# Experts: a product moved into each arm's end, flips of h in another order, one subtraction moved to GpSimd

## The chip, the cores and the metric

The kernel runs on one core of a Trainium2 chip. The metric is the device time of one execution in microseconds (us); three runs of the kernel before give the median that is compared. The engines are TensorE (PE, matmuls), VectorE (DVE), ScalarE (ACT), GpSimd (POOL) and SyncE (SP, which issues most transfers).

## The reference

Three stages in a row, on 1792 tokens of 768 columns: attention with a sigmoid in place of the softmax; a mixture of eight experts, of which each token takes one or none; a dense layer with 2048 hidden columns. The change is in the experts:

```python
do_compute = (x @ w_skip) > 0
xc = x[do_compute]
e_idx = np.argmax(xc @ w_gate, axis=1)
gate_w = probs[np.arange(len(xc)), e_idx]      # softmax of the same logits
for e in range(8):
    mask = e_idx == e
    h = np.maximum(xc[mask] @ w1[e], 0.0)      # w1[e]: 768 x 1024
    y[mask] = gate_w[mask, None] * (h @ w2[e]) # w2[e]: 1024 x 768
out[do_compute] = xc + y
```

## The kernel before

**Stages.** Attention runs to about 199 us, the routing of tokens to about 208, the experts to about 464, the dense layer to the end at 946 us.

**Blocks.** The tokens of each expert are cut into blocks of up to 256 rows, two halves of P = 128. How many blocks there are and how full they are is known only at run time: `level(i, k)` branches on `kinds`. k = 3 is a whole block (both halves), k = 2 a "few" block (one half and FEW = 64 rows), k = 1 one half; k = 0 ends the chain in `close`. The program holds all three arms for every level; the input takes the kinds 3, 3, 2, 3, 2, 1, 1, 1 for blocks 0 to 7 and then `close`. An arm that isn't taken is passed by `rest`, one small operation on each of PE, ACT and DVE, at the join.

**Weights.** Each block streams eight chunks of 128x1536 fp32: chunks 0 to 3 are w1 (the way up), 4 to 7 are w2 (back; c4 and c6 hold rows for the first 384 columns of the output, c5 and c7 for the last 384, c4 and c5 for the first half of h, c6 and c7 for the second). `split_w` cuts each chunk into a high part (a cast on ACT, L728) and a low part (the difference on DVE, L730), which go to one of four buffers, chunk c to buffer c modulo 4. `ahead(i, c)` splits chunk c + 2 while chunk c is used. A product of fp32 operands is then three matmuls (`gemm`, L737 to L739): high by high, high by low, low by high. For 64 rows it is two (L801, L802).

**One block.** `columns` flips the gathered rows (twelve matmuls L138) into two banks pt0, pt1 and acc1, from which ACT (L762) and DVE (L763) make the high and low part of x. In `between` come the previous block's products c5 and c6 for its first half, and in `lead_in` c7; then the up products, from which `h_columns` flips h (L138, or L778 for 64 rows), and ACT (L785) and DVE (L786) take the relu's high and low part. `back` runs the products c4 to c7 (twelve matmuls each for 128 rows, eight for 64), `outcome` scales and adds them (L916; for 64 rows after a fold by two matmuls, L915). Products of the first half that follow a block's own arm run in the next level, behind the next block's flips, so that PE has work there. `slot_order` (L1040 to L1054, block 0 alone) makes the row order that later gathers use.

**Order.** PE, ACT and DVE run the instructions in the order of the code (`manual_schedule`); GpSimd and SP, which issue gathers (L711), scatters (L928) and the weight transfers, are ordered by a scheduler. An engine waits for the others through semaphores.

Of the kernel before, what the change touches and what calls it, by code (L numbers as in the profile page):

```python
# [23 lines left out]
P = 128  # L24
# [10 lines left out]
KF1 = F1 // P  # L35
# [6 lines left out]
N2 = DM // 2  # L42
WCH = 1536
FA = 9
TB = 4
NOR = NTT // TB * TB
# [43 lines left out]
def build(nc, tc, a):  # L90
# [3 lines left out]
    with ExitStack() as top:  # L94
# [77 lines left out]
        with ExitStack() as st:  # L172
# [238 lines left out]
            raw = load(0, 0, True)  # L411
# [246 lines left out]
        with ExitStack() as st:  # L658
# [60 lines left out]
                    for h in range(2)  # L719
                ]  # L720

            def split_w(i, c, hi=True, lo=True):
                if i == NB:
                    return
                j = 8 * i + c
                raw, w_hi, w_lo = raw_t[j % NRAW], whi_t[j % NSPL], wlo_t[j % NSPL]
                if hi:
                    nc.scalar.copy(w_hi, raw)  # L728
                if lo:
                    nc.vector.tensor_sub(w_lo, raw, w_hi)  # L730

            def weights(i, c):
                j = (8 * i + c) % NSPL
# [34 lines left out]
                    split_columns(g, ends[g], x2)  # L768

            def h_columns(nh, sizes):  # L770
                for h, n in enumerate(sizes):
                    pt = pt_t[(nh + h) % 2].rearrange("p (c n) -> p c n", c=4)[:, :, :n]
                    for j in range(4):
                        w = slice(j * P, (j + 1) * P)
                        if n == P:
                            flip(pt[:, j, :], hs_t[nh][:, w])
                        else:
                            nc.tensor.matmul(  # L778
                                pt[:, j, :], hf_t[nh][:, w], fold[:, :n], start=True, stop=True
                            )  # L780
                    f, t = slice(4 * nh, 4 * nh + 4), slice(h * P, h * P + n)
                    h_hi, h_lo = h2[:, 0, f, t], h2[:, 1, f, t]
                    if n < P:
                        h_lo = h2[:, 0, f, h * P + n : (h + 1) * P]
                    nc.scalar.activation(h_hi, pt, AF.Relu)  # L785
                    nc.vector.scalar_tensor_tensor(  # L786
                        h_lo, pt, 0.0, h_hi, op0=ALU.max, op1=ALU.subtract
                    )

            def product(o, h, n, a2, i, c, width, k0, total):  # L790

                t = slice(h * P, (h + 1) * P)
                for j in range(WCH // width):
                    w = slice(j * width, (j + 1) * width)
                    hi, lo = (u[:, w] for u in weights(i, c))
                    a_hi, a_lo = a2[:, 0, k0 + j, t], a2[:, 1, k0 + j, t]
                    first, last = k0 + j == 0, k0 + j == total - 1
                    if n == P:
                        gemm(o, a_hi, a_lo, hi, lo, first, last)
                    else:  # L800
                        nc.tensor.matmul(o, a_hi, hi, start=first, stop=False, skip_group_check=True)  # L801
                        nc.tensor.matmul(  # L802
                            o[:n], a_hi[:, :n], lo, start=False, stop=last, skip_group_check=True
                        )
# [52 lines left out]
                        else:  # L857
                            nc.scalar.copy(hf_t[nh], acc_t[(3, 0)[nh]])

            def back(i, h, n, chunks):  # L860

                for c in chunks:
                    c4, nh = divmod(c - 4, 2)
                    product(py[nh][h], h, n, h2, i, c, N2, 4 * c4, KF1)
                    if n < P and c4:
                        nc.scalar.copy(yf_t[nh], py[nh][h])

            def expert(i, sizes, following=None):
                whole = sizes == (P, P)
                aside = places_in_order() if i == 0 else iter(())  # L870

                def soon():
                    if i:
                        outcome(i - 1, 0, P)

                if i == 0:
                    split_w(0, 1)
                if whole:
                    up_two(i, aside, soon)
                    ahead(i, 4)  # L880
                else:
                    up_parts(i, sizes, aside, soon)
                    if len(sizes) > 1:
                        skips(f"many{i}")
                    elif i + 1 < NB:
                        skips(f"more{i + 1}", (following + 3) >> 2)
                ahead(i, 5)
                if i == 0:
                    run(aside)
                    order_rows()  # L890
                for h, n in list(enumerate(sizes))[1:]:
                    if whole:
                        back(i, h, n, range(4, 8))
                        outcome(i, h, n)
                        back(i, 0, P, range(4, 5))
                    else:
                        back(i, h, n, range(4, 6))
                        h_columns(1, sizes)
                        back(i, h, n, range(6, 8))
                        back(i, 0, P, range(4, 5))  # L900
                        outcome(i, h, n)
                if i == 0:
                    slot_order()
                if len(sizes) == 1:
                    back(i, 0, P, range(4, 5))
                    h_columns(1, sizes)

            def outcome(i, h, n):

# [46 lines left out]
            def between(i, more):  # L956

                if i == 0 and more:
                    return
                if i == 1 and not more:  # L960
                    gather(1)
                columns(i)
                if i == 0:
                    return
                back(i - 1, 0, P, range(5, 7))
                if more:
                    split_w(i, 0)
                    split_w(i, 1)
                else:
                    back(i - 1, 0, P, range(7, 8))  # L970
                    outcome(i - 1, 0, P)
                    scatter(i - 1)
# [62 lines left out]

            def slot_order():

                og = acc_t[1][:, :NOR]
                for t in range(NOR):
                    nc.tensor.matmul(  # L1040
                        og, one_hot[:, t], ca[:, t], start=(t == 0), stop=(t == NOR - 1)
                    )
                nc.vector.tensor_copy(order_off, og)
                for j in range(4):
                    nc.vector.scalar_tensor_tensor(
                        slot_off,
                        fill[:, 3 - j : NHB + 7 - j],
                        order_off[:, j : j + 1],
                        slot_off,
                        op0=ALU.mult,  # L1050
                        op1=ALU.add,
                    )
                nc.vector.tensor_scalar_add(slot_ext, slot_off, float(NT))
                nc.vector.tensor_scalar_add(order, order_off, float(NT))  # L1054
# [24 lines left out]
                nc.vector.tensor_copy(next(rest_t[1]), cst[:, :1])  # L1079

            def level(i, k):
                pass_on(i)
                if i == NB:
                    close(i)
# [262 lines left out]
```

## Time and profile before

| | us |
|---|---|
| runs shown | 947.25, 949.8, 951.26 |
| median | 949.8 |
| the profiled execution | 948.0 |
| its span | 946.2 |
| PE busy | 910.7 (96%) |
| DVE busy | 585.6 (62%) |
| ACT busy | 504.6 (53%) |
| GpSimd busy | 72.3 (8%) |

Times in the rows are counted from the start of the span. The busy share of PE is an average over stages. In the rows below, "idle before <-releaser" is the time for which the engine stood ahead of that instruction, and what it was waiting for last; "issue" there is time in which it waited for nothing that the profile shows. A matmul's duration overlaps that of the next; the step from start to start is what it costs in a row of them.

### The profile page before, as it was taken

Reading aid. Unit: us, or ns where it says so; the run is one execution under the profiler, and the core shown is the slowest. Engines: PE = TensorE matmul, PEld = TensorE weight load, DVE = VectorE, ACT = ScalarE, POOL = GpSimd, SP = SyncE. Lnnn points to the kernel's source line nnn. Section 1 sums busy time; section 2 is a strip of 40 time slices with the busy share of each in tenths; the row PEclk is TensorE's granted clock in tenths of the full one; section 3 lists DMA queues with packets and bytes.
Section 4 is the critical chain, followed back from the end, with each engine's and each line's share of the span. In section 5 each row is a group of like instructions: output and inputs, shape, how many; then the busy total and the mean of one; then the engine's idle time right before and its main releaser. Section 6 shows DMA issues by size and latency. Waiting matters only on the chain.

```text
span 946.2 us, 13964 instructions
## 1 busy us (share of the span) xinstructions
PE 910.7 (96%) x5331; PEld 754.2 (80%) x5331; DVE 585.6 (62%) x893; ACT 504.6 (53%) x703; POOL 72.3 (8%) x69
## 2 busy tenths in 40 slices
PE   7999999999999999999799999999999999999998
PEld 4555555549997898888799999888888888888997
DVE  3787877957656456688388888533443444434664
ACT  7777777535345346577254455434443434443664
POOL 0000000010220110234100000000000100000100
PEclk9999999999999999999999999999999999999999
DMA  9989887579962683594663333000010100000100
GB/s 247 266 254 269 248 272 228 168 242 417 357 258 70 251 295 111 207 410 174 222 201 100 104 101 113 34 34 1 17 34 17 55 13 1 1 1 1 68 1 34
DMA packets 33992, 139.50 MB, mean 147 GB/s; under 512 B 4874, under 2 KB 5514, under 8 KB 33890
## 3 DMA queue, kind: packets, MB, share of 16 engines
q1 hardware_dynamic: 29410, 119.17, 37.8%
q0 software_dynamic: 4480, 19.01, 5.8%
q8 instruction: 59, 0.97, 0.4%
q14 instruction: 43, 0.35, 0.1%
HBM read 117.58 MB, written 23.60 MB: 149 GB/s over the span
## 4 chain that ended last, share of the span: by engine, by line
PE 83%; DVE 3%; issue 2%; ACT 2%; DMA 1%; SPq 0%; ACTq 0%; DVEq 0%
PE acc L1220 15%; PE pt L1220 9%; PE acc L1187 8%; PE acc L1188 8%; PE acc L1189 8%; PE acc L737 6%; PE acc L738 6%; PE acc L739 6%; PE ps L239 3%; PE po L253 3%; PE pt L138 1%; PE acc L801 1%; PE acc L802 1%; PE acc L138 1%; DMA raw<-in_wi 1%
## 5 line engine op out<-in xcount | busy, mean ns | idle before, releaser
L730 DVE TENSOR_TENSOR wlo<-raw,whi 128x1536 fp32r<-128x1536 f32 x64 | 111.3, 1756 | 34.6 <-ACT whi L728 34.2
L1198 DVE SCALAR_TENSOR_TENSOR m<-m,acc 128x512 f32<-128x512 f32 (+1 forms) x64 | 39.7, 621 | 143.9 <-ACT m L1197 143.9
L1196 ACT ACTIVATE m<-acc 128x512 f32<-128x512 f32 (+1 forms) x64 | 34.9, 546 | 171.5 <-PE acc L1189 171.5
L1187 PE MATMUL acc<-x,wih 128*128 128x256 f32 (+1 forms) x360 | 121.1, 336 | 0.0
L1188 PE MATMUL acc<-x,wih 128*128 128x256 f32 (+1 forms) x360 | 121.1, 336 | 0.0
L1189 PE MATMUL acc<-x,wil 128*128 128x256 f32 (+1 forms) x360 | 120.7, 335 | 0.0
L728 ACT CAST whi<-raw 128x1536 fp32r<-128x1536 f32 x64 | 94.0, 1482 | 25.0 <-DMA raw<-in_w 9.1
L246 ACT ACTIVATE at<-ps,bias 112x896 f32<-112x896 f32 x96 | 89.1, 1009 | 29.1 <-PE ps L239 29.1
L1220 PE MATMUL acc<-wol,gh 128*128 128x256 f32 x320 | 101.0, 316 | 0.0
L1220 PE MATMUL acc<-woh,gl 128*128 128x256 f32 x320 | 100.5, 314 | 0.0
L1220 PE MATMUL acc<-woh,gh 128*128 128x256 f32 x320 | 100.4, 314 | 0.0
L253 PE MATMUL po<-at,vt 112*64 112x448 f32 x384 | 77.5, 545 | 0.7 <-DVE xT L261 0.7
L239 PE MATMUL ps<-qs,kh 128*112 128x448 f32 x192 | 73.3, 382 | 3.0 <-ACT kh L232 1.5
L1177 DVE TENSOR_TENSOR wol<-wo,woh 128x768 fp32r<-128x768 f32 x64 | 61.2, 956 | 23.4 <-ACT woh L1176 23.0
L239 PE MATMUL ps<-qs,kl 128*112 128x448 f32 x192 | 71.6, 373 | 2.6 <-DVE kl L233 2.6
L1189 PEld LDWEIGHTS acc<-x,wil 128*128 128x128 f32 x360 | 68.0, 189 | 7.4
L1187 PEld LDWEIGHTS acc<-x,wih 128*128 128x128 f32 x360 | 68.0, 189 | 6.3
L1188 PEld LDWEIGHTS acc<-x,wih 128*128 128x128 f32 x360 | 67.9, 189 | 5.9
L1220 PEld LDWEIGHTS acc<-woh,gh 128*128 128x128 f32 x320 | 60.3, 188 | 10.1
L1220 PEld LDWEIGHTS acc<-wol,gh 128*128 128x128 f32 x320 | 60.3, 188 | 9.3
L1176 ACT CAST woh<-wo 128x768 fp32r<-128x768 f32 x64 | 53.4, 834 | 26.0 <-PE acc L1220 25.9
L1202 DVE TENSOR_TENSOR gl<-m,gh 128x512 fp32r<-128x512 f32 (+1 forms) x64 | 40.0, 626 | 40.5 <-ACT gh L1201 40.5
(252 smaller groups left out, 2034.7 us busy)
## 6 DMA issues: line engine op xcount, KB each, us to landing
raw<-in_w SPq DMA_DIRECT2D x66, 768.0 KB, 10.6
kr<-in_k SPq DMA_DIRECT2D x22, 448.0 KB, 6.7
raw<-in_wi SPq DMA_DIRECT2D x9, 768.0 KB, 6.8
raw<-in_wo SPq DMA_DIRECT2D x9, 768.0 KB, 6.5
vt<-in_v SPq DMA_DIRECT2D x12, 448.0 KB, 6.3
x_d<-xr SPq DMA_DIRECT2D x14, 384.0 KB, 3.4
raw<-in_wi SPq DMA_DIRECT2D x14, 384.0 KB, 3.1
raw<-in_wo SPq DMA_DIRECT2D x14, 384.0 KB, 3.1
```

What stands on the lines that cost most here:

```text
L239: nc.tensor.matmul(ps[:CP, j, :S], kk[:, 2 * p + j, c * CP : (c + 1) * CP], qs[:, p, j], start=(i == 0), stop=(i == 1),)
L246: nc.scalar.activation(at[:, :, c, :], ps[:CP, :, :S], AF.Sigmoid, bias=bias[:CP], scale=QK_SCALE)
L253: nc.tensor.matmul(po[64 * j : 64 * j + 64, :S], vt[:, 2 * (hp % 2) + j, c, :], at[:, j, c, :], start=(c == 0), stop=(c == NCH - 1),)
L728: nc.scalar.copy(w_hi, raw)
L730: nc.vector.tensor_sub(w_lo, raw, w_hi)
L737: nc.tensor.matmul(o, a_hi, b_hi, start=first, stop=False)
L738: nc.tensor.matmul(o, a_hi, b_lo, start=False, stop=False)
L1177: nc.vector.tensor_sub(pair[1], wo_r[f], pair[0])
L1187: nc.tensor.matmul(o, a, b, start=(cc == 0), stop=False)
L1188: nc.tensor.matmul(o, a, c, start=False, stop=False)
L1189: nc.tensor.matmul(o, wil[:, cc], b, start=False, stop=(cc == KD - 1))
L1220: nc.tensor.matmul(o, a, b, start=(clears and f == 0 and k_ == 0), stop=(f == KF2 - 1 and k_ == 2), skip_group_check=True,)
```

## The change

- In each arm, c5's product for the first half moves from `between` of the next level (behind the next block's flips) to the arm's end. `between` then has c6 alone; `lead_in` keeps c7. In a few block c5's matmuls stand half ahead of and half behind the two folds.
- `h_columns` goes through the halves in reversed order. In a few block it moves behind c4 of both halves, and c5 of the 64 rows follows it, where both c4 and c5 of the 64 rows stood ahead of it.
- `slot_order` runs ahead of c4 and c5 (whole) or right behind c4, and uses acc0.
- The low part of chunk 7 isn't made by DVE in the arm; GpSimd makes it at the start of the next level, ahead of that level's gathers and scatters. Only chunk 7's product for the first half comes behind it.

```diff
--- before.py
+++ after.py
@@ -719,7 +719,7 @@
                     for h in range(2)
                 ]
 
-            def split_w(i, c, hi=True, lo=True):
+            def split_w(i, c, hi=True, lo=nc.vector):
                 if i == NB:
                     return
                 j = 8 * i + c
@@ -727,7 +727,7 @@
                 if hi:
                     nc.scalar.copy(w_hi, raw)
                 if lo:
-                    nc.vector.tensor_sub(w_lo, raw, w_hi)
+                    lo.tensor_sub(w_lo, raw, w_hi)
 
             def weights(i, c):
                 j = (8 * i + c) % NSPL
@@ -768,7 +768,7 @@
                     split_columns(g, ends[g], x2)
 
             def h_columns(nh, sizes):
-                for h, n in enumerate(sizes):
+                for h, n in reversed(list(enumerate(sizes))):
                     pt = pt_t[(nh + h) % 2].rearrange("p (c n) -> p c n", c=4)[:, :, :n]
                     for j in range(4):
                         w = slice(j * P, (j + 1) * P)
@@ -787,10 +787,10 @@
                         h_lo, pt, 0.0, h_hi, op0=ALU.max, op1=ALU.subtract
                     )
 
-            def product(o, h, n, a2, i, c, width, k0, total):
+            def product(o, h, n, a2, i, c, width, k0, total, part=slice(None)):
 
                 t = slice(h * P, (h + 1) * P)
-                for j in range(WCH // width):
+                for j in range(WCH // width)[part]:
                     w = slice(j * width, (j + 1) * width)
                     hi, lo = (u[:, w] for u in weights(i, c))
                     a_hi, a_lo = a2[:, 0, k0 + j, t], a2[:, 1, k0 + j, t]
@@ -857,11 +857,11 @@
                         else:
                             nc.scalar.copy(hf_t[nh], acc_t[(3, 0)[nh]])
 
-            def back(i, h, n, chunks):
+            def back(i, h, n, chunks, part=slice(None)):
 
                 for c in chunks:
                     c4, nh = divmod(c - 4, 2)
-                    product(py[nh][h], h, n, h2, i, c, N2, 4 * c4, KF1)
+                    product(py[nh][h], h, n, h2, i, c, N2, 4 * c4, KF1, part)
                     if n < P and c4:
                         nc.scalar.copy(yf_t[nh], py[nh][h])
 
@@ -884,26 +884,31 @@
                         skips(f"many{i}")
                     elif i + 1 < NB:
                         skips(f"more{i + 1}", (following + 3) >> 2)
-                ahead(i, 5)
+                ahead(i, 5, lo=None)
                 if i == 0:
                     run(aside)
                     order_rows()
-                for h, n in list(enumerate(sizes))[1:]:
-                    if whole:
-                        back(i, h, n, range(4, 8))
-                        outcome(i, h, n)
-                        back(i, 0, P, range(4, 5))
-                    else:
-                        back(i, h, n, range(4, 6))
-                        h_columns(1, sizes)
-                        back(i, h, n, range(6, 8))
-                        back(i, 0, P, range(4, 5))
-                        outcome(i, h, n)
+                start, end = slice(0, 2), slice(2, 4)
+                if whole:
+                    back(i, 1, P, range(4, 8))
+                    outcome(i, 1, P)
+                    if i == 0:
+                        slot_order()
+                    back(i, 0, P, range(4, 6))
+                    return
+                if len(sizes) > 1:
+                    back(i, 1, sizes[1], range(4, 5))
+                back(i, 0, P, range(4, 5))
                 if i == 0:
                     slot_order()
-                if len(sizes) == 1:
-                    back(i, 0, P, range(4, 5))
-                    h_columns(1, sizes)
+                h_columns(1, sizes)
+                if len(sizes) > 1:
+                    back(i, 1, sizes[1], range(5, 8))
+                    back(i, 0, P, range(5, 6), start)
+                    outcome(i, 1, sizes[1])
+                    back(i, 0, P, range(5, 6), end)
+                else:
+                    back(i, 0, P, range(5, 6))
 
             def outcome(i, h, n):
 
@@ -962,7 +967,7 @@
                 columns(i)
                 if i == 0:
                     return
-                back(i - 1, 0, P, range(5, 7))
+                back(i - 1, 0, P, range(6, 7))
                 if more:
                     split_w(i, 0)
                     split_w(i, 1)
@@ -1035,7 +1040,7 @@
 
             def slot_order():
 
-                og = acc_t[1][:, :NOR]
+                og = acc_t[0][:, :NOR]
                 for t in range(NOR):
                     nc.tensor.matmul(
                         og, one_hot[:, t], ca[:, t], start=(t == 0), stop=(t == NOR - 1)
@@ -1079,6 +1084,8 @@
                 nc.vector.tensor_copy(next(rest_t[1]), cst[:, :1])
 
             def level(i, k):
+                if i:
+                    split_w(i - 1, 7, hi=False, lo=nc.gpsimd)
                 pass_on(i)
                 if i == NB:
                     close(i)
```

In the rows of the order below wloN, whiN are the four buffers for the low and high parts of a chunk, rawN the loaded chunks, pt0, pt1, acc0 to acc5 the banks, xgNN a block's rows, h2 and x2 the two parts of h and x. L1086 and L1093 of the kernel before are L1093 and L1100 of the changed one.

DVE, arm of one half, block 5, its end and the start of the next level; before:

```order
L730 TENSOR_TENSOR wlo0_1893<-raw5_1873,whi0_1892 128x1536
L730 TENSOR_TENSOR wlo1_1891<-raw6_1874,whi1_1890 128x1536
L786 SCALAR_TENSOR_TENSOR h2_1869<-pt0_1958,h2_1869 128x4x128
L730 TENSOR_TENSOR wlo2_1889<-raw7_1875,whi2_1888 128x1536
L730 TENSOR_TENSOR wlo3_1887<-raw8_1876,whi3_1886 128x1536
L786 SCALAR_TENSOR_TENSOR h2_1869<-pt1_1959,h2_1869 128x4x128
L1093 UNCONDITIONAL_BRANCH
L1086 COMPARE_AND_BRANCH
L763 TENSOR_TENSOR x2_1868<-pt0_1958,x2_1868 128x512
```

and now:

```order
L730 TENSOR_TENSOR wlo0_1893<-raw5_1873,whi0_1892 128x1536
L730 TENSOR_TENSOR wlo1_1891<-raw6_1874,whi1_1890 128x1536
L786 SCALAR_TENSOR_TENSOR h2_1869<-pt0_1958,h2_1869 128x4x128
L730 TENSOR_TENSOR wlo2_1889<-raw7_1875,whi2_1888 128x1536
L786 SCALAR_TENSOR_TENSOR h2_1869<-pt1_1959,h2_1869 128x4x128
L1100 UNCONDITIONAL_BRANCH
L1093 COMPARE_AND_BRANCH
L763 TENSOR_TENSOR x2_1868<-pt0_1958,x2_1868 128x512
```

The subtraction into wlo3 behind that into wlo2 is gone, and the second L786 follows the one into wlo2.

PE, few arm, block 2, its end; before:

```order
L737 MATMUL acc2_1962<-whi0_1892,h2_1869 128x384
L738 MATMUL acc2_1962<-wlo0_1893,h2_1869 128x384
L739 MATMUL acc2_1962<-whi0_1892,h2_1869 128x384
L915 MATMUL acc0_1960<-hf0_1883,cst_79 128x384
L915 MATMUL acc1_1961<-hf1_1884,cst_79 128x384
L1096 UNCONDITIONAL_BRANCH
```

and now:

```order
L737 MATMUL acc4_1964<-whi1_1890,h2_1869 128x384
L738 MATMUL acc4_1964<-wlo1_1891,h2_1869 128x384
L739 MATMUL acc4_1964<-whi1_1890,h2_1869 128x384
L920 MATMUL acc0_1960<-hf0_1883,cst_79 128x384
L920 MATMUL acc1_1961<-hf1_1884,cst_79 128x384
L737 MATMUL acc4_1964<-whi1_1890,h2_1869 128x384
L738 MATMUL acc4_1964<-wlo1_1891,h2_1869 128x384
L739 MATMUL acc4_1964<-whi1_1890,h2_1869 128x384
L737 MATMUL acc4_1964<-whi1_1890,h2_1869 128x384
L738 MATMUL acc4_1964<-wlo1_1891,h2_1869 128x384
L739 MATMUL acc4_1964<-whi1_1890,h2_1869 128x384
L1103 UNCONDITIONAL_BRANCH
```

The products into acc4 are c5's, which stood in the next level; six of them follow the folds, ahead of the branch out of the arm.

GpSimd, behind block 5's arm, the start of the next level; before:

```order
L1093 UNCONDITIONAL_BRANCH
L928 DMA x_d_60<-xg00_1894,slot_tok_83 1793x768
L1069 TENSOR_LOAD kinds_99
L1086 COMPARE_AND_BRANCH
L711 DMA xg00_1894<-x_d_60,slot_ext_84 128x768
L711 DMA xg01_1895<-x_d_60,slot_ext_84 128x768
L928 DMA x_d_60<-xg11_1897,slot_tok_83 1793x768
```

and now:

```order
L1100 UNCONDITIONAL_BRANCH
L730 TENSOR_TENSOR wlo3_1887<-raw8_1876,whi3_1886 128x1536
L933 DMA x_d_60<-xg00_1894,slot_tok_83 1793x768
L1074 TENSOR_LOAD kinds_99
L1093 COMPARE_AND_BRANCH
L711 DMA xg00_1894<-x_d_60,slot_ext_84 128x768
L711 DMA xg01_1895<-x_d_60,slot_ext_84 128x768
L933 DMA x_d_60<-xg11_1897,slot_tok_83 1793x768
```

The subtraction comes first, and the scatter of block 4 and the gathers queue behind it.

## Rows read from the trace of the kernel before

**Rows 1.** Busy time by stage: engines' busy us (count), PE clock, DMA share, GB/s.

```profile
208.00:464.00 256.00, 239.29 (x1485) 220.40 (x1483) 166.96 (x197) 134.24 (x157) 45.84 (x34) 0.99 0.67 254
464.00:946.20 482.20, 477.44 (x2844) 423.50 (x2844) 262.72 (x425) 226.38 (x377) 18.55 (x19) 1.00 0.16 50
```

**Rows 2.** PE's waits, 208 to 467 us: for whom, us, times, longest.

```profile
PE pt L138 <- DVE h L786: 4.4, 3, 1.5
PE acc L1187 <- issue: 3.9, 1, 3.9
PE pt L138 <- issue: 2.1, 1, 2.1
PE acc L801 <- DVE h L786: 1.9, 2, 0.9
PE pt L138 <- DVE order L1054: 1.3, 1, 1.3
PE pt L138 <- DVE rest L1079: 1.0, 1, 1.0
```

**Rows 3.** DVE timeline, block 0's end: start, us, engine line op [idle before].

```profile
242.91 1.11 DVE L1045 SCALAR_TENSOR_TENSOR slot_off<-fill,order_off,slot_off 128x32 f32<-128x32 f32 x4
```

**Rows 4.** DVE timeline, middle of block 2.

```profile
304.33 1.76 DVE L730 TENSOR_TENSOR wlo<-raw,whi 128x1536 fp32r<-128x1536 f32 x1 [2.01 <-ACT whi L728]
306.21 1.05 DVE L786 SCALAR_TENSOR_TENSOR h<-pt,h 128x512 fp32r<-128x512 f32 x2
```

**Rows 5.** PE timeline, start of block 5.

```profile
388.32 1.09 PE L138 MATMUL pt<-cst,xg 128*128 128x128 f32 x8 [1.01 <-DVE rest L1079]
...
389.61 0.42 PE L737 MATMUL acc<-whi,h 128*128 128x384 f32 x1
```

**Rows 6.** PE timeline, block 6 between its flips and those of block 7.

```profile
409.51 0.66 PE L138 MATMUL pt<-cst,xg 128*128 128x128 f32 x4 [1.46 <-DVE h L786]
...
410.36 0.42 PE L737 MATMUL acc<-whi,h 128*128 128x384 f32 x1
...
416.73 0.39 PE L737 MATMUL acc<-whi,x 128*128 128x512 f32 x1
...
425.56 0.34 PE L737 MATMUL acc<-whi,h 128*128 128x384 f32 x1
...
430.17 0.66 PE L138 MATMUL pt<-cst,xg 128*128 128x128 f32 x4 [1.46 <-DVE h L786]
```

**Rows 7.** DVE timeline, the same block.

```profile
412.69 3.43 DVE L730 TENSOR_TENSOR wlo<-raw,whi 128x1536 fp32r<-128x1536 f32 x2 [0.58 <-ACT whi L728]
...
418.21 1.14 DVE L916 SCALAR_TENSOR_TENSOR xg<-acc,slot_gate,xg 128x384 f32<-128x384 f32 x2
419.27 3.41 DVE L730 TENSOR_TENSOR wlo<-raw,whi 128x1536 fp32r<-128x1536 f32 x2
423.12 1.76 DVE L730 TENSOR_TENSOR wlo<-raw,whi 128x1536 fp32r<-128x1536 f32 x1 [0.44 <-ACT whi L728]
424.79 0.68 DVE L786 SCALAR_TENSOR_TENSOR h<-pt,h 128x512 fp32r<-128x512 f32 x1
...
427.75 1.76 DVE L730 TENSOR_TENSOR wlo<-raw,whi 128x1536 fp32r<-128x1536 f32 x1 [0.34 <-ACT whi L728]
429.43 0.68 DVE L786 SCALAR_TENSOR_TENSOR h<-pt,h 128x512 fp32r<-128x512 f32 x1
```

**Rows 8.** The view of rows 1, start of block 3.

```profile
316.00:320.00 4.00, 4.00 (x20) 4.00 (x20) 2.21 (x4) 3.03 (x4) 0.00 (x0) 0.62 0.92 310
```

**Rows 9.** GpSimd (POOL) timeline: two casts, two scatters.

```profile
16.97 0.72 POOL L429 CAST tri_b<-early_cst 128x128 bf16<-128x128 f32 x1 [15.18 <-DMA early_cst<-in_consts]
17.64 0.28 POOL L430 CAST iota_h<-early_cst 128x128 f16<-128x128 f32 x1
...
406.86 1.00 POOL L928 DMA_INDIRECT x_d<-xg,slot_tok  x1 [5.60 <-DVE wlo L730]
...
419.45 2.46 POOL L928 DMA_INDIRECT x_d<-xg,slot_tok  x1 [0.31 <-DVE xg L916]
```

## What is predicted, and why

> **What bounds the kernel now.** I read the busy time by stage first [rows 1]. The final dense stage keeps TensorE (PE) busy for 477.4 of its 482.2 us, and the diff doesn't touch it. The expert stage, 208 to 464 us, has 239.3 us of PE in 256.0, at a granted clock of 0.99: 16.7 us of idle time are the most that this change can reach. So the second view is PE's waits in that stage [rows 2]. It is a list of stalls on VectorE (DVE), not on transfers: 4.4 us in three waits for `h_columns` (L786) behind the blocks of one half, 1.9 us in two waits for the same line inside the two blocks of one half and 64 rows, 1.3 us for `order` (L1054) at the end of block 0, 1.0 us for DVE's `rest` (L1079) at the end of block 4. These make 8.6 us. Beside them stand two stretches of "issue", 2.1 us at the end of block 2 and 3.9 us at the end of the stage, in which PE waits for nothing that the profile shows. Third, the DVE rows around the waits [rows 3, 4, 7] say why DVE is late there: at each of the `h_columns` waits a subtraction L730 of 1.76 us, the low part of chunk 7, stands directly ahead of the L786 that PE needs, though chunk 7 itself is wanted only later.
>
> On this data the eight blocks are of the kinds whole, whole, few, whole, few, one, one, one (blocks 0 to 7), then the close. Each kind is costed apart.
>
> **Blocks of one half (5, 6, 7).** Before, PE ends the arm with the flips of h, flips part of the next columns, and stands for 1.46 us until L786 is through [rows 6]. From flip to flip the period is 430.17 - 409.51 = 20.66 us. The change puts c5's 12 products behind the flips of h. 36 products took 416.73 - 410.36 = 6.37 us [rows 6], so 12 take 2.12, and that is longer than the wait even if lo7 stayed on DVE. All three waits (4.4 us) go. What is late next? Behind the flips only 24 products (4.25 us) are left ahead of the first up product, not 36. PE reaches c4 4.25 + 8.83 (416.73 to 425.56) us after its first product, and c4's third matmul, which reads h's low part, 0.35 later: at 13.43. DVE starts lo0 2.33 after the same point (412.69 against 410.36), and then has six subtractions in a row (two take 3.43 [rows 7], so each adds 1.67), the pair L916 (1.06 net of overlap) and L786 (0.68): 2.33 + 10.02 + 1.06 + 0.68 = 14.09. Before, the same L786 ended at 425.47, just ahead of c4 at 425.56. So a **new wait of about 0.65 us** stands ahead of c4's third matmul in every such block; DVE, not PE, sets that stretch. Its bounds: 0 if the chain packs tighter, 1.1 if lo5 also waits 0.44 for its cast, as it did [rows 7]. Net 1.46 - 0.65 = 0.81 a block, **2.4 us** for three.
>
> lo0 is another near miss: it is done 2.33 + 1.76 = 4.09 after the first product, and wanted at 4.25 plus one matmul. Cover is 0.2 to 0.3 us.
>
> **Mid of the few blocks (2, 4).** DVE ran lo7 (304.33 to 306.09) and then two L786 in 1.05 us [rows 4], and PE waited 1.9 us in the two blocks [rows 2]. Now lo7 is gone from DVE, the 64-row half is flipped and taken first, and c5's eight matmuls (8 x 0.177 = 1.4 us) stand between the flips and c6, which reads it. 1.4 us and the four flips of the other half cover one relu and one L786. I take **1.87 us** off; cover left is about 0.5 us.
>
> **End of the few blocks.** The two fold matmuls move ahead of c5's last six products, so DVE's L921 pair and `rest` start 1.06 us sooner against PE; the wait of 1.01 at block 4 [rows 2] goes, barely. But GpSimd's new subtraction stands behind the join of the arm: it starts about 0.3 us after the arm's end, and c7's second matmul needs it after 12 flips (388.32 to 389.61, 1.29 us [rows 5]), 12 products of c6 (2.12) and one matmul: at 3.6. With the duration G taken below, 0.1 to 0.9 us are missing; I take 0.4. Net **0.6 us**. At block 2 the end has the 2.1 us of issue, followed by a stretch at 0.62 of the clock [rows 8]; the profile doesn't say what PE does in it, and if it hangs on where the code behind the branch lies, the order doesn't tell it either. I leave it as it is; it hides the subtraction there. Blocks 1 and 3 have no wait in rows 2, so nothing is to be had there.
>
> **Block 0.** `slot_order` moves ahead of 24 products (4.25 us), which cover the chain of small DVE operations, four of which alone take 1.11 us [rows 3] and for which PE stood 1.3 us [rows 2]. The products that hide it are c4 and c5 of the first half; without that cover the wait would be back. Four of these operations (L1045) may meet GpSimd's subtraction in time. I take **1.0 us** of the 1.3.
>
> **GpSimd's subtraction (8 new, of 128x1536).** No row shows one. Its nearest rows are two casts of 128x128 on GpSimd, 0.72 us for the first and 0.28 for the second [rows 9]. Twelve times these are 8.6 and 3.4 us; DVE's own 1.76 is the lower bound. I take G = 3.4 to 4.2, nearest to the second cast (the first one follows 15 us of idle), and keep the ends for the range.
>
> The Trainium skill (GPSIMD Engine Reference, 3.1 Elementwise) gives 4497 ns for such an operation of 2048 elements, 1.96 times DVE's; that would be an estimate of 3.4 us here, and the sum stays. No run so far shows it.
>
> Where does it lie? The products of chunk 7 for a second half (whole and few blocks) now run ahead of it, with what its buffer still holds, chunk 3's low part; so they wait for nothing, and only the first half's products use the new result. In whole blocks (0, 1, 3) it starts when c7's products of the second half end, and is wanted 24 products, 12 flips, 12 products and one matmul later, 4.25 + 1.29 + 2.12 + 0.18 = 7.8 us: hidden. In blocks of one half it waits for lo6 and the relu of h, 0.75 us after the flips of h, and is wanted 2.12 + 1.29 + 2.12 + 0.18 = 5.7 after them: hidden by 0.7 to 1.5 us. On GpSimd's own queue it stands ahead of the scatter and the gathers of later rows (L928, L711); these were issued a level ahead, so a few us more there reach nobody. SP's loads of weights that reuse chunk 7's raw buffer now wait for GpSimd, not for DVE one queue later; no wait of PE in rows 2 is put down to a transfer, so I cost that at nothing. Cover gone, it would show as PE or ACT waiting for DMA at L728.
>
> **Sum.** 2.4 + 1.9 + 0.6 + 1.0 = 5.9 us. The profiled execution took 948.0 us (span 946.2), 1.8 under the median of 949.8; so 942.1 there, **943.9 against the median**. A measurement of this kernel can't tell less than about 0.5% from no change, so faster is below 945.1 and slower above 954.5.
>
> **Rivals.**
> (a) *All waits go.* DVE packs tighter, GpSimd is in time: 8.6 us, or 10.7 if the issue at block 2's end goes too: 939 to 941. For it: DVE has idle time in every block. Against: rows 7 are nearly back to back, so the 0.65 us have to be paid.
> (b) *DVE takes the gain back.* lo0 misses its 0.2 us, or is held by GpSimd; h's low part is 1.1 us late. A DVE rule may do that: in the trace a GpSimd transfer of 1.00 us takes 2.46 when it begins inside a DVE subtraction [rows 9], so the two engines do hold each other up. If DVE's lo0 has to wait for the subtraction's end in the few blocks and in those of one half, 0.5 us more go in each of five, and with 1.1 for 0.65 the gain is 5.9 - 2.5 - 1.4 = 2.0: 947.8.
> By the Trainium skill (SBUF — State Buffer, Who interferes with whom) a DVE instruction with two SBUF inputs contends with a GpSimd one that reads SBUF, and whoever issues first holds the other off for the whole instruction; the 2.46 us row is in line with it, though that is a transfer. It speaks against a subtraction on GpSimd beside those on DVE, and is what (b) would be.
> (c) *GpSimd is slow.* Then c7's product waits in the close and each later lead-in: G - 3.3 in two few blocks, G - 4.9 in three blocks of one half. The gain is used up from G = 5.5, and it is slower by over 0.5% from G = 6.5 (5G - 21.3 against 6.3 + 4.7). At 8.6 us it costs 10.6 + 11.1 + 2.4 (whole blocks) and gives about 968. For it: GpSimd's first cast at 0.72 us for 128 elements. Against: the second at 0.28.
> (d) *The layout of the code decides.* PE's "issue" gaps follow branches; the code before them moves by some 60 instructions a level. One more or one fewer stretch like the one at block 2, with its half-clock tail, is 3.5 us either way: 940.4 or 947.4.
> (e) *The order is not what it says.* In the built order c5 stands in the arm and lo7 is off DVE in every arm, so I give this nothing.
>
> **How the numbers follow.** Forecast 0.42 (941.5 to 947, some three quarters of it below 945.1), (a) 0.12, (b) 0.22, (c) 0.12, (d) 0.12, half each way. Faster: 0.32 + 0.12 + 0.06 = 0.50. Slower: (c) 0.12, and 0.01. Same: the rest, 0.37. The range reaches from 938.5, the full gain, to 952, which leaves out most of (c) and no more.
>
> **What would show it.** Right: no PE wait for L786 ahead of flips, none for `order`; in blocks 5 to 7 a PE wait at L739 of 0.5 to 1.1 us for DVE's L786; GpSimd's L730 rows of 3 to 4.5 us; a flip-to-flip period near 19.8. Wrong: PE waits at L738 for GpSimd's `wlo`, or at the first up product for DVE's `wlo` (then (b) or (c)); L730 rows on DVE well over 1.76 us; "issue" gaps at other branches (d).

## The result, and the profile after

The changed kernel takes 953.66 us (median of 8 runs, 948.48 to 957.96) against 948.14 us (8 runs, 946.58 to 951.26): ratio 1.0058, 95% interval 1.004 to 1.0076. It is slower by 0.6%, where 943.9 had been forecast. The profiled execution took 953.85 us, its span 952.1, against 946.2 before.

PE's waits in the expert stage and the first of the dense stage, changed kernel (what waited, for whom: us in total, times, longest), against [rows 2]:

```profile
PE acc L737 <- issue: 4.7, 1, 4.7
PE acc L737 <- DVE rest L1084: 3.5, 2, 1.9
PE acc L1082 <- issue: 2.5, 1, 2.5
PE acc L1196 <- issue: 2.3, 1, 2.3
PE pt L138 <- issue: 2.2, 2, 1.8
PE acc L739 <- DVE h L786: 1.0, 2, 0.6
```

Every wait that the change aims at is gone: `order`, both in the few blocks, all three ahead of the flips, `rest` at block 4's end (an issue gap of 1.78 us stands in its place in this profile; in the changed kernel with 64 instructions added, below, neither does). What it was expected to add is there too, 1.0 us at L739 for L786. But two things stand in their place that the sum did not have: a second wait for DVE's `rest` (1.55 of the 3.5 us; the other 1.92 is before block 0 in both kernels), and issue: 11.8 us in these rows, against 6.4 before (6.0 in [rows 2] and one of 0.4).

The issue gaps show in PE's sequencer as long branches. Branch instructions of PE by line, 208 to 470 us, count and min/median/max ns. They are, in order, the branches `more`, `two`, `few` and `many` of `level`; first the kernel before:

```profile
L1086 PEldq COMPARE_BRANCH  x9: 68/73/6190, 241.6 to 457.9; - x9
L1093 PEldq COMPARE_BRANCH  x7: 67/68/1952, 246.8 to 432.6; - x7
L1096 PEldq COMPARE_BRANCH  x7: 66/222/431, 209.7 to 384.5; - x7
L1100 PEldq COMPARE_BRANCH  x10: 63/192/3501, 210.2 to 385.2; - x10
```

and the same four of the changed kernel, 7 lines further down in the code:

```profile
L1093 PEldq COMPARE_BRANCH  x9: 68/73/3866, 245.4 to 463.6; - x9
L1100 PEldq COMPARE_BRANCH  x7: 68/68/7140, 249.3 to 440.2; - x7
L1103 PEldq COMPARE_BRANCH  x7: 66/211/4912, 212.3 to 389.2; - x7
L1107 PEldq COMPARE_BRANCH  x10: 63/250/3351, 212.7 to 389.9; - x10
```

Most take some tens or hundreds of ns. The kernel before has two long ones, 3.5 and 6.2 us, at its two issue gaps; `two` and `few`, at most 1.95 and 0.43 us there, now reach 7.1 and 4.9. The 7.1 us are the branch from `between` to the arm of one half in block 5, during which PE ran out of work (the products issued ahead of the branch run on for 2.5 us, so the gap is the shorter of the two):

```profile
402.06 0.51 PE L737 MATMUL acc<-whi,h 128*128 128x384 f32 x1 [4.69 <-issue]
```

and in the stretch 398 to 402 us, the DMA view has one packet of code of this kind (queue, kind: packets, MB, share):

```profile
q8 instruction: 1, 0.02, 1.5%
```

One packet says little by itself: 28 such packets of 16 KB pass between 208 and 464 us in either kernel. But each branch of PE of over 2 us, two to eight a profile and 62 in the twelve profiles with branches, ends 1.3 to 1.5 us behind the end of one (here 400.60, branch to 402.01). So the long branches can be read as waits for code. The 2.32 us gap in the dense stage has no branch in it, and ends 1.3 us behind such a packet as well.

Behind some of these gaps the clock falls to the lower of its two levels (behind that of 1.78 us it doesn't): TensorE's granted clock is 0.65 and 0.57 of full in the 4 us behind the gaps at 327 and 402 us (the last three figures are clock, DMA share, GB/s; [rows 8] is the same of before).

```profile
326.00:330.00 4.00, 2.76 (x13) 2.71 (x14) 1.05 (x1) 2.56 (x2) 0.00 (x0) 0.65 1.00 398
402.00:406.00 4.00, 3.94 (x13) 3.93 (x14) 1.05 (x2) 0.00 (x0) 1.08 (x2) 0.57 1.02 422
```

Where the 5.9 us between the two profiled executions lie, from the start of each block's up products (read from PE's timelines, difference after less before):

| stretch | us | what is in it |
|---|---|---|
| up to block 0's up products | +1.0 | code that the change doesn't touch |
| block 0 | +2.9 | the first products at half the clock (+2.6), `rest` (+1.55), `order` (-1.28) |
| block 1 | -0.2 | |
| block 2 | -1.5 | -0.93 for L786; issue 2.1 and half clock before, 0.46 and 2.52 now |
| block 3 | +1.5 | half clock behind the 2.52 us gap |
| block 4 | +5.9 | issue 1.78 and 4.69 and half clock; -1.95 of waits |
| blocks 5, 6, 7 with the close | -6.4 | -4.4 for L786 and -4.3 of issue; +1.0 at L739, +1.6 for ACT at the end (a branch of 3.87 us ends there 0.08 us behind ACT's cast) |
| dense stage | +2.5 | a new issue gap of 2.3, half clock in both |

### The profile page after: what moved, and what is told of

Its sections match the earlier page's. It is cut to its first block, busy times and chain, and to the rows that moved or that the text cites. A ratio compares the mean times of both kernels' runs of the same rounds, so it can differ in the third digit from the quotient of the medians.

```text
span 952.1 us, 13973 instructions
## 1 busy us (share of the span) xinstructions
PE 913.0 (96%) x5331; PEld 757.4 (80%) x5331; DVE 574.2 (60%) x885; ACT 502.7 (53%) x703; POOL 98.9 (10%) x77
## 4 chain that ended last, share of the span: by engine, by line
PE 79%; DVE 3%; DMA 3%; issue 3%; ACT 2%; SPq 0%; ACTq 0%; DVEq 0%
PE acc L1227 15%; PE pt L1227 9%; PE acc L1194 8%; PE acc L1196 8%; PE acc L1195 8%; PE acc L737 5%; PE acc L739 5%; PE acc L738 5%; PE ps L239 3%; PE po L253 3%; PE pt L138 1%; PE acc L801 1%; PE acc L802 1%; DVE wlo L730 1%; PE acc L138 1%
## 5 line engine op out<-in xcount | busy, mean ns | idle before, releaser
L1194 PE MATMUL acc<-x,wih 128*128 128x256 f32 (+1 forms) x360 | 121.7, 338 | 0.0
L730 DVE TENSOR_TENSOR wlo<-raw,whi 128x1536 fp32r<-128x1536 f32 x56 | 96.6, 1754 | 24.0 <-ACT whi L728 23.5
L1194 PEld LDWEIGHTS acc<-x,wih 128*128 128x128 f32 x360 | 68.7, 191 | 6.2
L737 PE MATMUL acc<-whi,h 128*128 128x384 f32 x176 | 61.7, 351 | 4.7 <-issue 4.7
```

Of the source, the lines that this page charges most:

```text
L730: lo.tensor_sub(w_lo, raw, w_hi)
L737: nc.tensor.matmul(o, a_hi, b_hi, start=first, stop=False)
L1194: nc.tensor.matmul(o, a, b, start=(cc == 0), stop=False)
```

## The experiments

Theories after the result. **L**: the issue gaps, and the half clock behind them, come where PE branches into code that isn't there yet, and at which branch that happens hangs on where the code lies; the change moves all code behind it. **S**: they come from the change itself, which leaves PE less work between two branches. **A** and **B**: two causes for the late `rest`. Medians and ratios are each against the kernel before on the same chip.

### e1: block 0's low part back on DVE

```diff
-                ahead(i, 5, lo=None)
+                ahead(i, 5, lo=nc.vector if i == 0 else None)
...
-                if i:
+                if i > 1:
                     split_w(i - 1, 7, hi=False, lo=nc.gpsimd)
```

> The changed kernel, but for block 0 the low part of chunk 7 is again made by DVE in the arm (the seven other blocks keep GpSimd); PE's program is the same, instruction for instruction. Theory A (the four L1050 of slot_order were held behind GpSimd's subtraction, 0.86 us each for 0.28, and that makes DVE's rest late at block 1): the 1.55 us wait for rest at block 1's start goes to under 0.3, L1050 is back at 0.28 us. Rival B (rest is late for another reason, the two subtractions lo0 and lo1 ahead of it): the wait stays at 1.3 to 1.6 us. On the issue gaps: if they belong to where PE's code lies (theory L), this kernel shows them in the same places as the changed kernel, 2.5 us at block 3's rest, 1.8 and 4.7 us around block 5's start, 2.3 us in the dense stage; if they are chance from run to run (theory R), in other places. Time under L and A: 1 to 1.6 us below the changed kernel, 1.004 to 1.005 of the kernel before.

951.88 us (9 runs), ratio 1.0049 (1.0029 to 1.0068). First the DVE row of the changed kernel with GpSimd's row beside it, then DVE's row of e1:

```profile
243.70 3.50 POOL L730 TENSOR_TENSOR wlo<-raw,whi 128x1536 fp32r<-128x1536 f32 x1 [34.61 <-DMA raw<-in_w]
244.57 3.54 DVE L1050 SCALAR_TENSOR_TENSOR slot_off<-fill,order_off,slot_off 128x32 f32<-128x32 f32 x4
```

```profile
241.62 1.11 DVE L1050 SCALAR_TENSOR_TENSOR slot_off<-fill,order_off,slot_off 128x32 f32<-128x32 f32 x4
```

Without the subtraction on GpSimd the four take 1.11 us, with it 3.54, to 0.9 us past its end at 247.20. It is the first of the four that stands, for 2.68 us up to that end; the others take 0.25 each. So the hold-up is real; but PE's waits in e1 say that it cost nothing:

```profile
PE acc L737 <- issue: 4.1, 1, 4.1
PE acc L737 <- DVE rest L1084: 3.5, 2, 1.9
PE acc L1082 <- issue: 2.6, 1, 2.6
```

The wait for `rest` at block 1 is 1.56 as before: A falls, B stays. The time went the way that was expected under A, but the intervals of the two kernels overlap, so it tells nothing between A and B. And the issue gaps are in the same places (4.13, 2.61, 1.65 and 2.18 us against 4.69, 2.52, 1.78 and 2.32): against chance from run to run. Block 0's first products run at full clock in this profile, so their half clock in the changed kernel's profile isn't due to where PE's code lies.

### e2: GpSimd's subtraction alone

```diff
-                ahead(i, 5)
+                ahead(i, 5, lo=None)
...
             def level(i, k):
+                if i:
+                    split_w(i - 1, 7, hi=False, lo=nc.gpsimd)
```

> The kernel before with one part of the change: GpSimd makes the low part of chunk 7 at the start of the next level (chunk 7's products of a second half then use what the buffer still holds, the low part of chunk 3). PE's program stays that of the kernel before, instruction for instruction. Theory L (code placement makes the issue gaps): gaps as before, 2.1 us at block 2's end and 3.9 us at the end of the stage, none new. Theory A for the gain: L786 no longer stands behind lo7, so the three waits behind the blocks of one half shrink from 1.46 to about 0.9 us each (the relu is the later one then) and the two in the few blocks from 0.93 to 0.2 to 0.9; GpSimd's 3.5 us are hidden behind 24 products. Time: 2 to 4 us below the kernel before, ratio 0.996 to 0.998. Theory G (the work on GpSimd itself is what costs the changed kernel its time): ratio 1.002 or more.

945.09 us (12 runs), ratio 0.9965 (0.9951 to 0.9978): faster by 3.4 us. So it isn't the work on GpSimd that costs the changed kernel its time (theory G of the expectation falls). PE's waits:

```profile
PE pt L138 <- DVE h L786: 2.9, 3, 1.0
PE acc L801 <- DVE h L786: 1.9, 2, 0.9
PE pt L138 <- issue: 1.8, 1, 1.8
PE pt L138 <- DVE order L1054: 1.8, 1, 1.8
```

Behind the blocks of one half it is 0.98 each for 1.46. In the few blocks 0.93 is left whole: there the relu and two L786 behind the flips were late by themselves, and lo7, which stood ahead of them, wasn't what PE waited for. `order` grew from 1.28 to 1.82, the hold-up that e1 showed, here on the path. The 3.9 us of issue at the end of the stage are missing in this profile (a wait of 1.5 us for ACT stands there), though PE's program is that of the kernel before. The branch there is long all the same, 3.80 us for 6.19, and ends at 460.73, within 0.01 us of ACT's cast: its packet of code set out 1.5 us after the branch began, before it was 3.8 us. So of the gain the shorter waits for L786 are 1.5 us, less 0.5 for `order`, and 2.4 us are this shorter stop (3.89 to 1.52), which no wait for DVE explains.

### The placement of the code, six kernels

64, 128 and 192 instructions of PE (32, 64 and 96 of these matmuls) in block 0's arm for one half, which this input never takes, in either kernel:

```diff
                         expert(i, (P,), following)
+                        if i == 0:
+                            for _ in range(64):
+                                nc.tensor.matmul(
+                                    acc_t[5][:, :2], iota_h, iota_h[:, :2], start=True, stop=True
+                                )
```

> The changed kernel with 64 small matmuls (128 instructions of PE) put into the arm of block 0 that this input never takes: nothing more is executed, all code behind that arm lies 128 instructions further. Theory L: the issue gaps move: some of the four (2.5, 1.8, 4.7, 2.3 us) go, others come, and the time moves by some us, down to about 944 if most go. Theory S (the gaps come from the change itself, which leaves only c6's 12 products and 12 flips, 3.4 us, between two branches of PE): gaps of the same size at the same branches, time within 1 us of the changed kernel.

> The kernel before with the same 128 instructions in the arm never taken. Theory L: its two issue gaps (2.1 us at block 2's end, 3.9 us at the end of the stage) move to other branches or change in number, and the time changes by 2 to 6 us either way against the kernel before, although no executed instruction differs. Theory S: no change, ratio within 0.998 to 1.002.

> The changed kernel with 64 instructions of PE in the arm of block 0 that is never taken. Theory L: other issue gaps than at 0 and 128 instructions (12.0 and 15.5 us in sum in their profiles); the time lies anywhere from 944 (next to no gap) to 958. Theory S (the gaps come from the change's shorter way between branches): a sum of 10 us or more again, and 952 or more.

> The kernel before with 64 instructions of PE in the arm of block 0 that is never taken. Theory L: between 948 (no added gap) and 960 (as with 128 instructions), with gaps at other branches. Theory S: 948 to 949, since the order of the kernel before has room; that is already against its 960 at 128 instructions.

> The same with 192 instructions. Theory L: again another set of gaps, 944 to 958. Theory S: a sum of 10 us or more, 952 or more. Over the four placements theory L has the changed kernel's mean not above that of the kernel before over its placements.

> The kernel before with 192 instructions of PE in the arm of block 0 that is never taken; with it both kernels stand at four placements. Theory L: anywhere from 948 to 960, its issue gaps 6 to 13 us in sum; the mean of the kernel before over its four placements (948.1, 957.8, 960.3 so far) is then about 955 to 956, at or above the mean of the changed kernel over its four (953.7, 947.9, 956.8, 959.4: 954.5). Theory S: 948 to 949.

| instructions added | before, us | issue, us | after, us | issue, us |
|---|---|---|---|---|
| 0 | 948.1 | 6.4 | 953.7 | 12.0 |
| 64 | 957.8 | 12.6 | 947.9 | 9.1 |
| 128 | 960.3 | 13.0 | 956.8 | 15.5 |
| 192 | 956.9 | 11.0 | 959.4 | 15.8 |
| mean | 955.8 | 10.8 | 954.5 | 13.1 |

("issue" is the sum of PE's gaps in one profile, from 204 us on. Beside it the changed kernel has 1.6 to 1.9 us at the stage's end that the profile puts down to ACT, where a branch of 3.9 to 4.2 us ends 0.1 to 0.4 us behind ACT's cast.) No executed instruction differs, and the kernel before moves by 12 us, ratio 1.0128 (1.0112 to 1.0145) at 128; the changed one between ratio 1.0002 (0.9984 to 1.002) and 1.0114 (1.01 to 1.0129). S falls for the kernel before, which was to stay at 948 to 949: it stands at its best placement of four as it is, and has gaps elsewhere as soon as it is moved. Its waits at 128 (L1192 and L1194 are in the dense stage):

```profile
PE acc L1192 <- issue: 4.1, 1, 4.1
PE acc L737 <- issue: 3.7, 1, 3.7
PE acc L1077 <- issue: 2.8, 1, 2.8
PE acc L1194 <- issue: 2.4, 1, 2.4
```

and those of the changed kernel at 64, its best:

```profile
PE acc L737 <- issue: 5.1, 3, 3.4
PE acc L737 <- DVE rest L1084: 3.5, 2, 1.9
PE acc L1082 <- issue: 2.4, 1, 2.4
PE pt L138 <- issue: 1.6, 1, 1.6
```

Over four placements the two means differ by 1.3 us in favour of the change. Something of S may be left: the changed kernel has 2.3 us more of issue on the mean, with four placements too few to tell that from chance.

### e5: chunk 1 split in the taken arm

```diff
-                if i == 0:
-                    split_w(0, 1)
+                split_w(i, 1)
...
                     split_w(i, 0)
-                    split_w(i, 1)
```

> The changed kernel, but chunk 1 of the next block (cast and low part) is split at the start of the taken arm, not ahead of the branch; PE's program is unchanged, instruction for instruction. Theory B (DVE's rest stands behind lo0 and lo1, and with 12 products fewer ahead of the up products PE now arrives first): the 1.55 us wait for DVE's rest at block 1's start goes, as rest is done one subtraction (1.67 us) sooner; at block 3 the wait is hidden in an issue gap of 2.5 us, which stays. The other gaps stay at the places of the changed kernel (theory L). Time: 1 to 2 us below the changed kernel, 1.003 to 1.005 of the kernel before. Rival: lo1 starts late behind the branch and the second up chunk waits for it, 0.5 us or more at three whole blocks: no gain.

948.86 us (12 runs), ratio 1.001 (0.9998 to 1.0023), for 1.0058. First the changed kernel's DVE rows at block 1 with PE's beside them:

```profile
251.86 3.43 DVE L730 TENSOR_TENSOR wlo<-raw,whi 128x1536 fp32r<-128x1536 f32 x2 [0.46 <-ACT whi L728]
255.20 0.14 DVE L1084 COPY rest<-cst 128x1 f32<-128x1 f32 x1
```

```profile
255.49 0.35 PE L737 MATMUL acc<-x,whi 128*128 128x256 f32 x1 [1.55 <-DVE rest L1084]
```

`rest` stands behind lo0 and lo1, PE arrives 4.5 us after its first product and stands. In e5 it is ahead of lo1, and the wait is gone (1.92 is block 0's):

```profile
PE acc L737 <- issue: 4.7, 1, 4.7
PE acc L1080 <- issue: 2.5, 1, 2.5
PE acc L737 <- DVE rest L1082: 1.9, 1, 1.9
```

The issue gaps stay where they were, as L had it. B holds. The gain is larger than the 1 to 2 us expected, 4.8 us by the medians (4.6 by the ratios). The two profiled executions differ by 3.7 us (952.1 to 948.4), of which 1.55 is `rest` and 1.75 lies ahead of block 0's up products, in code that is the same in both; so I count `rest` alone as shown.

### The straight kernels

Both kernels with the arms written out for this input's kinds, without `tc.If` and `rest` (right for this input alone):

```diff
-                with tc.If(k > 0, label=f"more{i}") as more:
...
+                between(i, True)
+                fetch(i + 1, range(2))
+                lead_in(i)
+                expert(i, {1: (P,), 2: (P, FEW), 3: (P, P)}[KINDS[i]], 0)
+                level(i + 1, 0)
```

> The kernel before as straight code for the kinds that this input has (3, 3, 2, 3, 2, 1, 1, 1, then the close): the arms that are never taken, the branches and rest are left out, so it is right for this input alone; the work on the taken path is the same. Theory L (the issue gaps and the half-clock stretches behind them come from branches into code that is not loaded): no issue gap of 1 us or more in the expert stage; the waits of the order itself stay, 1.3 for order, 0.9 twice and 1.46 three times for L786. Time about 948.1 - 6.4 (issue) - 3.4 (half clock) - 2.9 (rest) = 936, range 933 to 942. If the gaps are not from branches: above 945.

> The changed kernel as straight code in the same way. This takes code placement and rest out of the comparison. Theory L with the working of the prediction: of the waits only L739 for L786 in the blocks of one half stay (0.3 to 0.65 us each); the waits for order, for L786 in the few blocks and for L786 ahead of the flips are gone. Time 6 to 7 us under the straight kernel before, so about 929.5. Theory S (the change itself lengthens the way): equal to the straight kernel before within 2 us, or above it.

936.79 us (4 runs), ratio 0.988 (0.9866 to 0.9894), and 931.93 us (5 runs), ratio 0.9817 (0.9802 to 0.9832). All of PE's waits in the expert stage, first of the kernel before, then of the changed one (0.7 for L762 is at the stage's end):

```profile
PE pt L138 <- DVE h L786: 3.3, 3, 1.5
PE acc L1175 <- ACT x L762: 0.7, 1, 0.7
PE acc L801 <- DVE h L786: 1.9, 2, 0.9
PE acc L738 <- DVE x L763: 0.3, 1, 0.3
```

```profile
PE acc L739 <- DVE h L786: 1.3, 3, 0.5
PE acc L738 <- POOL wlo L730: 0.4, 1, 0.4
PE acc L738 <- DVE x L763: 0.3, 1, 0.3
```

No issue gap is left in either, and the kernel before is 11.7 us faster without branches (and without the 2.9 us of waits for `rest`). Neither has a long branch of PE any more, and 12 packets of code for 28 pass in the same stretch. There the change is worth 4.9 us by the medians and 4.2 by the waits (6.2 less 2.0); the 6 to 7 expected were too many since `order` is no wait in the straight kernel, and L786 behind the last block is 0.34 instead of 1.48.

### e5_pad64: the best of both

> The changed kernel with both: chunk 1 split in the taken arm, and 64 instructions of PE in the arm never taken, the placement with the smallest sum of issue gaps for the changed kernel (9.1 us). Theory B with L: the 1.56 us wait for DVE's rest at block 3 goes, the gaps stay where they are with 64 instructions; 1.5 to 3 us under that kernel's 947.9, so 945 to 946.5, ratio 0.997 to 0.9985 of the kernel before. If other waits take its place: 947.5 or more.

e5 with 64 instructions added takes 946.09 us (11 runs), ratio 0.9978 (0.9964 to 0.9993): faster than both kernels, though less so than e2 (0.9965), which keeps the placement of the kernel before. PE's issue waits:

```profile
PE acc L737 <- issue: 6.2, 3, 4.9
PE pt L138 <- issue: 1.9, 1, 1.9
PE acc L1080 <- issue: 1.5, 1, 1.5
```

The 1.56 us for `rest` at block 3 are gone, the gaps stand at the same branches.

## Why the prediction was wrong, step by step

- **Blocks of one half: right.** All three waits of 1.46 went, and the new one stands where the sum of DVE's chain put it, at c4's third matmul: 0.35 and 0.64 us in blocks 6 and 7 for the 0.65 worked out, none in block 5, whose start was late anyway. From flips to flips it is 19.8 us, as worked out.

```profile
434.77 0.44 PE L739 MATMUL acc<-whi,h 128*128 128x384 f32 x1 [0.35 <-DVE h L786]
454.60 0.44 PE L739 MATMUL acc<-whi,h 128*128 128x384 f32 x1 [0.64 <-DVE h L786]
```

- **Mid of the few blocks: right in size, wrong in cause.** 1.87 us went, but e2 shows that taking lo7 off DVE does nothing there; it must be the order of the halves or c5 behind the flips, which no run here parted.
- **End of the few blocks: half right.** `rest` at block 4 is no wait any more. GpSimd's 0.4 us don't show: at block 2 the subtraction ends 0.45 us ahead of c7's second matmul (322.10 and 322.55), and at block 4 an issue gap of 4.69 us lies over it. The 0.39 us for `wlo` in the straight kernel stand elsewhere, behind block 5 of one half, which had been taken as hidden by 0.7 to 1.5: there a gather went ahead of the subtraction on GpSimd, and it began only at 404.23, 0.56 us behind the flips, where in the changed kernel it begins 1.2 us ahead of them.
- **GpSimd: right.** G was taken as 3.4 to 4.2 us from the second of the casts in [rows 9]; the eight take 3.44 to 3.50. Rival (c) falls. The estimate of 3.4 us from the Trainium skill's page (GPSIMD Engine Reference, 3.1 Elementwise) is borne out, and so is the rule of its page SBUF — State Buffer (Who interferes with whom): an operation of DVE with two SBUF inputs stood until GpSimd's was through (the 2.68 us of e1's comparison).
- **Block 0: right**, 1.28 for the 1.0 taken.
- **Blocks 1 and 3: wrong.** The step that failed is the sentence that there was nothing in them "to be had", because they had no wait. I held lo0 against the shorter way to the up products (4.09 against 4.25) and not `rest`, which in a whole block stands behind lo0 and lo1: 2.33 + 3.35 + 0.14 = 5.8 against 4.25 and a branch. That is 1.55 us at block 1, and at block 3 the same where no issue gap covers it (1.56 at 64 and at 128 instructions). It is off by 1.6 to 3.1 us, and the change's doing (e5).
- **Placement: wrong, and the larger part.** I kept the two issue gaps as they were and gave rival (d) 0.12, at 3.5 us. I wrote that the profile doesn't say what PE does in the gap at block 2's end; it does, in the rows of PE's branches: L1100 takes 3.50 us there. The change moves every branch of the expert stage, and its profile has 5.6 us more of issue and more products at half the clock behind it (block 3 is 1.5 us longer by that alone). The price of one gap was about right (2.52 and 1.5 us at block 3), the number of them was not: moving the code alone costs the kernel before 8 to 12 us. I took its two gaps for its share in any placement, while it stands at the best of the four tried.

The Trainium skill (Runtime: NRT & Kernel Launch, Instruction fetch mechanics) says that a taken branch whose target isn't in the window of code at hand has to wait for a page to be fetched. I didn't weigh it; the 62 branches that end behind a packet of code, and the straight kernels, agree with it. It would have made the forecast open by some 10 us on the slow side.

So the change is worth some 4 to 5 us where code placement is out of the comparison; the forecast's terms without those for `rest` and `order`, which are no waits there, come to 3.9 (2.4 + 1.9 - 0.4). As it is built it loses more than that at PE's branches and for `rest` at block 1. What stays open is the rule by which a given branch misses: the same branch (behind `between` in block 5) costs 4.7, 3.4, 4.6 and 1.7 us at four placements, the same last branch took 6.2 us in one profile and 3.8 in e2's, and no run here varied the prefetch hints or the traffic beside a code packet.

## What to carry to other kernels

In a program with branches at run time, look at PE's branch instructions by line before and after an edit: if the longest is microseconds and the median is 70 ns, then code placement can be part of the time, and an edit has to be judged over several placements (unused instructions in an arm that is never taken), or on a straight version. And when work is taken out from between two points, hold every instruction that stands between them on every other engine against the shorter way, the small ones at a join (`rest`) as well as the large.

## What the runs showed of the hardware beyond that

- 64 to 192 instructions that never run moved the time by up to 1.3% (948.1 to 960.3 us).
- The half clock behind a wait of PE does not come in each execution of the same PE program: block 0's first 27 products took 6.05 us for 3.42 in the changed kernel's profile, behind waits of 1.1 and 1.9 us, and ran at full clock in e1's behind 0.6 and 1.9. The changed kernel's runs spread over 9.5 us, those of the kernel before over 4.7.
